# First two groups of a causal convolution on TensorE: x as the stationary operand in 128x32 tiles, written already transposed, and a reordered second bundle

## The chip, the cores and the metric

The kernel runs on one NeuronCore of a Trainium2 chip. The metric is device microseconds of one execution. TensorE is called PE in the profile (PEld is its weight load), VectorE DVE, ScalarE ACT, GpSimd POOL and SyncE SP.

## The reference

The input x is 8 sequences of 4160 tokens with 192 channels, in fp32. Two things are computed one after the other.

```python
# 1. a causal depthwise convolution of 7 taps; the 24 channels of a head share its softmaxed taps
w = softmax(weight, axis=-1)                       # (8 heads, 7)
y[b, s, h*24+g] = sum_k w[h, k] * x[b, s-6+k, h*24+g]
# 2. a channel mix on y
y_prev = y shifted by one token
xk = mu_k*y + (1-mu_k)*y_prev ;  xr = mu_r*y + (1-mu_r)*y_prev
k  = relu(xk @ w_k)            # 192 -> 1024
v  = (k*k) @ w_v               # 1024 -> 192
r  = sigmoid(xr @ w_r)         # 192 -> 192
out = r * v
```

## The kernel before

**Pairs and channels.** The eight sequences go in four pairs. In the transposed activations (`yT`) the 128 partitions hold 64 channels of the one sequence and 64 of the other, so that the 192 channels are three chunks c of 64 (`Q`), and the tokens run along the free dimension.

**Convolution.** Tokens go in blocks of 120. With 126 rows of x behind it, a block's output for one head is a product with a banded 128x128 matrix `toe[:, h, :]`, which holds the softmaxed taps. Blocks are gathered in groups. Pair 0 has groups 0 to 5 of 3, 4, 4, 5, 10 and 9 blocks; the other pairs have four groups each. For all groups the banded matrix is PE's stationary operand (lhsT) and x streams past it, so the result has tokens on the partitions and has to be transposed:

- groups 0, 1 and 2 are convolved by `conv_small`: 10 matmuls (L321), each for one head's part of one chunk, then three casts out of PSUM (L329) into `y_small`. `tr_first` (group 0, L414 to L422) and `tr` (groups 1, 2 and 3, L390) transpose 120x120 blocks on PE and copy them into `yT` (L417, L420, L400);
- group 3 is convolved in two units (`conv_mm`, L300, and `conv_out`, L345), and transposed by `tr` too;
- all later groups are written to DRAM and read back transposed by DMA (`y_write`, `y_read`).

**Channel mix.** A pair's tokens go in steps; pair 0 starts with a step of 256 tokens (step 0), then seven of 512. For a step, DVE forms `d` (`diff`, L444), and from it xk and xr (`scale` L475 and `add_y` L481; in step 0 xk is one L457 for each chunk). A slot n is `k_mm` (L501; six matmuls of 64x512, three chunks by two sequences, or in step 0 twelve of 64x256), `k_relu` on ACT (L530) and `k_square` on DVE (L544). Four slots are a bundle: bundle 0 is step 0, bundles 1 and 2 are step 1, and so on. From bundle 2 on each bundle also has one `r` (L575 and a sigmoid, L583) and one quad of the V product in two halves (`v_rows`, L603), with the product `v_out` (L619) and its DMA.

**Order.** It is written out by hand: each engine runs its instructions in the order in which the program calls them. `prologue` loads, builds `toe` and convolves groups 0 and 1; `bundle_first` is bundle 0; `bundle_rest` is every other bundle. Work that accompanies a bundle hangs in tables by bundle number (`first`, `mix_a`, `mix_b`, `mix_c`, `rq`, `xt`, `late`, `early`). All PSUM tiles are of two banks and come from one ring of four (`ring`): a tile can be taken when one of the last four has been read out. In `conv_mm` and `v_rows` an empty ACT instruction (`clobber_nop`, L308, L611) after the first half keeps ACT from going on before that half is done. x comes through POOL's DMA queue into three buffers `xb`.

Of the kernel before, what the change touches and what calls it, by code (L numbers as in the profile page):

```python
# [7 lines left out]
FP32 = mybir.dt.float32  # L8
# [6 lines left out]
def kernel(  # L15
# [293 lines left out]

    def conv_small(g, copies):  # L310

        nb = groups[g][2]
        ys[g] = [two.tile([P, 4, P], BF16, tag=f"y_small{i}", name="y_small") for i in range(NC)]
        tiles = [ring.tile([P, 2, BANK], FP32, tag="k", name="ps_c") for _ in range(3 if g == 0 else 2)]
        banks = [t[:, i, 0 : nb * P] for t, i in ((tiles[0], 0), (tiles[1], 0), (tiles[-1], 0 if g == 0 else 1))]
        for i, o in enumerate(banks):
            o = o.rearrange("p (n s c) -> p n s c", n=nb, s=2)
            c0, c1 = i * Q, (i + 1) * Q
            for h in range(c0 // G, -(-c1 // G)):
                a, b = max(c0, h * G), min(c1, h * G + G)  # L320
                nc.tensor.matmul(  # L321
                    out=o[:, :, :, a - c0 : b - c0],
                    lhsT=toe[:, h, :],
                    rhs=xbs[g][:, :nb, :, a:b],
                    start=True,
                    stop=True,
                )
        for i, o in enumerate(banks):
            copies[i](out=ys[g][i][:BLK, :nb, :].rearrange("p n c -> p (n c)"), in_=o[:BLK, :])  # L329

# [50 lines left out]
    def tr(g, j):  # L381
# [14 lines left out]
        for i in todo[::2]:  # L396
            n = min(2, nb - i)
            c0 = YC + (blk0 + i) * BLK
            copy = nc.scalar.copy if g == 1 and i > 0 else nc.vector.tensor_copy
            copy(  # L400
                out=yTs[p][:, :, c0 : c0 + n * BLK].rearrange("p c (n t) -> p c n t", n=n),
                in_=view[:, (i - 4 * j) // 2, :, :n, :],
            )

    def tr_first():

        nb = groups[0][2]
        n = nb * BLK
        new_yT(0)
        tiles = [ring.tile([P, 2, 2 * BANK], BF16, tag="k", name="ps_t") for _ in range(2)]  # L410
        for c in range(3):
            for i in range(nb):
                c0 = c % 2 * n + i * BLK
                nc.tensor.transpose(  # L414
                    out=tiles[1 - c // 2][:, 0, c0 : c0 + BLK], in_=ys[0][c][:BLK, i, :], identity=ident[:BLK, :BLK]
                )
        nc.scalar.copy(out=yTs[0][:, 2, YC : YC + n], in_=tiles[0][:, 0, 0:n])  # L417
        for c in range(3):
            if c < 2:
                nc.vector.tensor_copy(out=yTs[0][:, c, YC : YC + n], in_=tiles[1][:, 0, c * n : (c + 1) * n])  # L420
            diff(0, slice(c, c + 1))
            mix(0, 0, slice(c, c + 1))  # L422

# [61 lines left out]
    def k_mm(n, cs=range(NC)):  # L485
# [10 lines left out]
        for c in cs:  # L496
            for f in range(nf):
                fs = slice((j * nf + f) * P, (j * nf + f + 1) * P)
                for i in range(2):
# [7 lines left out]
                    )  # L507

    def k_section(ns):
        s, _ = slots[ns[0]]  # L510
        if ns[0] > 0:
            for n in ns:
                k_mm(n)
            return
        for n in ns:
            k_ps[n] = ring.tile([P, 2, BANK], FP32, tag="k", name="ps_k")
            if n == 0:

                warm(k_ps[0], 3)
        for c in range(NC):  # L520
            if c == NC - 1:
                run(first, 0)
            for n in ns:
                k_mm(n, (c,))

# [124 lines left out]

    early, first, rq, xt, mix_a, mix_b, mix_c, vq, late = ({} for _ in range(9))

    def at(table, b, fn, *a):
        table.setdefault(b, []).append((fn, a))

    def conv(g, c):
        act_, dve_ = nc.scalar.copy, nc.vector.tensor_copy
        conv_small(g, (act_, act_, dve_ if g == 0 else act_))

# [6 lines left out]
    for g, (p, blk0, nb, fb, on_pe) in enumerate(groups):  # L666
        nx = 1 if g < 3 else len(conv_units(g))
        if g == 0:
            continue
        if g == 1:  # L670
            xs = []
        elif p == 0:
            xs = {2: [0], 3: [1, 1], 4: [2, 2, 3, 3], 5: [4, 4, 5, 5]}[g]
        else:
            xs = range(fb - 10, fb - 10 + nx)
        for i, b in enumerate(xs):
            if g == 2:
                at(late, b, conv, g, i)
            else:
                xt.setdefault(b, []).append((g, i))  # L680
        if on_pe:
            for j in range((nb + 3) // 4):
                at(first, g - 1, tr, g, j)
        else:
            at(late, xs[-1], y_write, g)

            at(late, xs[-1] + (1 if g < 6 else 2), y_read, g)
        if g > 4:

            b = {5: 1, 6: 2, 7: 7}.get(g)  # L690
            b = first_bundle[first_step[p]] + (-15, -11, -7, -3)[(g - 6) % 4] if b is None else b
            at(early, b, x_tile, g)
            at(early, b, load_x, g)
    for s, (p, t0, L, n0, ns) in enumerate(steps):
        fb = first_bundle[s]
        if s == 0:
            at(mix_c, 1, mix, s, 1)
            continue
        if s == 1:
            at(mix_a, 0, diff, s)  # L700
            at(mix_a, 0, mix, s, 0)
            at(mix_a, 1, scale, s, 1, 0)
            at(mix_b, 1, scale, s, 1, 1)
            at(late, 2, scale, s, 1, 2)
            at(late, 2, add_y, s, 1)
        else:
            if s == 2:
                at(mix_b, 1, diff, s)
            elif s == 4:
# [31 lines left out]
    def prologue():  # L741
# [33 lines left out]
        load_mu(1, moe_mu_r)  # L775
        conv(0, 0)
        tr_first()
        conv(1, 0)
        x_tile(3)
        load_x(3)  # L780
        load_wr()
        x_tile(4)
        load_x(4)
        load_wv()

    def bundle_first(ns):
        for part in (ns[:2], ns[2:]):
            k_section(part)
            for n in part:
                k_relu(n)  # L790
        run(mix_a, 0)
        for n in ns:
            k_square(n)
        run(late, 0)

    def bundle_rest(b, ns):

        units = xt.get(b, []) + [None, None]
        quad = vq.get(b, [None])[0]
        for n in bundles[b - 1][2:] if b > 1 else ():  # L800
            k_square(n)
        run(mix_a, b)
        k_mm(ns[0])
        k_relu(ns[0])
        run(first, b)
        k_square(ns[0])
        run(mix_b, b)
        conv_half(units[0], 0)
        k_mm(ns[1])
        conv_half(units[0], 1)  # L810
        k_relu(ns[1])
        k_square(ns[1])
        run(rq, b)
        if quad:
            v_rows(*quad, 0)
        k_mm(ns[2])
        k_relu(ns[2])
        conv_half(units[1], 0)
        if quad:
            v_rows(*quad, 1)  # L820
            conv_half(units[1], 1)
        run(mix_c, b)
        k_mm(ns[3])
        if not quad:
            conv_half(units[1], 1)
# [5 lines left out]
    with tc.manual_schedule():  # L831
        prologue()
        for b in range(-20, 0):
            for table in (early, first, rq, xt, mix_a, mix_b, mix_c, vq, late):
                assert b not in table, b
        for b in range(quads[-1][2] + 1):
            run(early, b)
            if b == 0:
                bundle_first(bundles[b])
            elif b < len(bundles):  # L840
                bundle_rest(b, bundles[b])
# [39 lines left out]
```

## Time and profile before

| what | us |
|---|---|
| median of 3 runs | 422.44 (422.27 to 422.84) |
| the profiled execution, as timed | 422.14 |
| its span in the trace | 420.4 |
| PE busy | 409.8 (97%) |
| DVE busy | 380.9 (91%) |
| ACT busy | 347.5 (83%) |

Busy shares are of the span. PE's ends are modelled, so that busy time is time with matmuls in flight. In the groups, a line shows the busy time, the mean of one instruction, and the idle time in front of them with what ended it.

### The profile page before, as it was taken

Reading aid. Unit: us, or ns where it says so; the run is one execution under the profiler, and the core shown is the slowest. Engines: PE = TensorE matmul, PEld = TensorE weight load, DVE = VectorE, ACT = ScalarE, POOL = GpSimd, SP = SyncE. Lnnn points to the kernel's source line nnn. Section 1 sums busy time; section 2 is a strip of 40 time slices with the busy share of each in tenths; the row PEclk is TensorE's granted clock in tenths of the full one; section 3 lists DMA queues with packets and bytes.
Section 4 is the critical chain, followed back from the end, with each engine's and each line's share of the span. In section 5 each row is a group of like instructions: output and inputs, shape, how many; then the busy total and the mean of one; then the engine's idle time right before and its main releaser. Section 6 shows DMA issues by size and latency. Waiting matters only on the chain.

```text
span 420.4 us, 15787 instructions
## 1 busy us (share of the span) xinstructions
PE 409.8 (97%) x6845; PEld 315.7 (75%) x6845; DVE 380.9 (91%) x677; ACT 347.5 (83%) x408; POOL 49.0 (12%) x73
## 2 busy tenths in 40 slices
PE   8789999999999999999999999999999999999995
PEld 3456777777977787777778777877777788777795
DVE  5899889998999999999999999999999999999973
ACT  5788988988888898889888888988898788787771
POOL 7650010202020010202003010201100000000000
PEclk9999999999999999999999999999999999999999
DMA  8996869969599793868769794696856484421123
GB/s 131 192 190 113 217 173 146 227 189 164 165 169 217 152 223 99 139 188 183 182 114 201 167 203 126 140 234 150 160 139 133 138 153 121 118 77 53 64 79 113
DMA packets 134886, 64.58 MB, mean 154 GB/s; under 512 B 85132, under 2 KB 134816, under 8 KB 134816
## 3 DMA queue, kind: packets, MB, share of 16 engines
q1 hardware_dynamic: 96050, 48.31, 45.3%
q0 software_dynamic: 37872, 14.66, 30.4%
q8 instruction: 53, 0.87, 0.8%
q10 hardware_dynamic: 894, 0.61, 0.5%
q14 instruction: 17, 0.14, 0.1%
HBM read 29.92 MB, written 36.99 MB: 159 GB/s over the span
## 4 chain that ended last, share of the span: by engine, by line
PE 90%; ACT 2%; DVE 1%; issue 0%; ACTq 0%
PE ps_v L603 39%; PE ps_k L501 38%; PE ps_r L575 7%; PE ps_c L300 4%; ACT k_sb L530 2%; PE ps_v L558 1%; DVE o_sb L619 0%; ACT y L345 0%; DVE k L544 0%; DVE yT L400 0%; DVE d L444 0%; DVE xr L475 0%; PE ps_t L390 0%; DVE o_sb L639 0%; ACTq L345 0%
## 5 line engine op out<-in xcount | busy, mean ns | idle before, releaser
L530 ACT ACTIVATE k_sb<-ps_k 128x1024 bf16<-128x1024 f32 x260 | 261.3, 1040 | 52.5 <-PE ps_k L501 52.5
L501 PE MATMUL ps_k<-xk,wk 64*128 64x512 bf16 (+1 forms) x1632 | 201.0, 367 | 1.5 <-ACT k_sb L530 0.5
L544 DVE TENSOR_TENSOR k<-k_sb 128x1024 bf16<-128x1024 bf16 x260 | 177.6, 687 | 14.9 <-ACT k_sb L530 7.8
L603 PE MATMUL ps_v<-wv,k 64*128 64x192 bf16 x4032 | 188.8, 243 | 0.2 <-ACT y L345 0.2
L603 PEld LDWEIGHTS <-k 64*128 64x128 bf16 x4032 | 172.5, 94 | 13.2 <-issue 0.7
L501 PEld LDWEIGHTS <-wk 64*128 64x128 bf16 x1632 | 87.8, 94 | 52.2 <-issue 2.5
L619 DVE TENSOR_TENSOR o_sb<-ps_v,r_sb 128x768 f32<-128x768 f32 x64 | 61.2, 956 | 11.9 <-PE ps_v L603 5.0
L583 ACT ACTIVATE r_sb<-ps_r 128x768 bf16<-128x768 f32 x65 | 54.7, 845 | 0.0
L345 ACT CAST y<-ps_c 120x960 bf16<-120x960 f32 (+4 forms) x67 | 50.9, 789 | 4.5 <-PE ps_c L300 4.5
L125 POOL DMA_DIRECT2D xb<-in_x_dram x34 | 30.7, 905 | 195.3 <-PE ps_c L300 129.3
L575 PEld LDWEIGHTS <-xr 64*128 64x128 bf16 x780 | 35.9, 94 | 11.3 <-DVE yT L400 0.4
L575 PE MATMUL ps_r<-wr,xr 64*128 64x192 bf16 x780 | 43.8, 243 | 0.0
L300 PE MATMUL ps_c<-xb,toe 64*128 64x480 bf16 (+2 forms) x240 | 39.5, 335 | 0.1
L475 DVE TENSOR_SCALAR xr<-d,mu 128x512 bf16<-128x512 bf16 (+1 forms) x102 | 35.5, 351 | 0.0
L475 DVE TENSOR_SCALAR xk<-d,mu 128x512 bf16<-128x512 bf16 (+1 forms) x99 | 32.6, 358 | 0.1
L481 DVE TENSOR_TENSOR xr<-xr,yT 128x1536 bf16<-128x1536 bf16 (+1 forms) x33 | 31.0, 939 | 1.1
L444 DVE TENSOR_TENSOR d<-yT 128x1536 bf16<-128x1536 bf16 (+2 forms) x35 | 31.0, 887 | 1.0 <-ACT yT L400 0.8
L481 DVE TENSOR_TENSOR xk<-xk,yT 128x1536 bf16<-128x1536 bf16 (+1 forms) x32 | 30.2, 942 | 0.0
L300 PEld LDWEIGHTS <-toe 64*128 64x128 bf16 x240 | 13.4, 94 | 12.2 <-DVE o_sb L619 0.5
L428 POOL COPY y_tail<-yT 128x195 bf16<-128x195 bf16 x4 | 1.8, 458 | 68.5 <-DMA yT<-y_dram 68.5
L739 PE MATMUL warm<-zeros,ones_t 128*128 128x512 bf16 x16 | 6.5, 594 | 1.8 <-DVE zeros L754 1.8
L739 PEld LDWEIGHTS <-ones_t 128*128 128x128 bf16 x19 | 2.6, 135 | 5.6 <-issue 4.0
(55 smaller groups left out, 63.9 us busy)
## 6 DMA issues: line engine op xcount, KB each, us to landing
out_dram<-o_sb SPq DMA_DIRECT2D x128, 192.0 KB, 2.6
y_dram<-y SPq DMA_DIRECT2D x10, 900.0 KB, 6.7
xb<-in_x_dram POOLq DMA_DIRECT2D x14, 480.0 KB, 9.1
xb<-in_x_dram POOLq DMA_DIRECT2D x6, 432.0 KB, 7.6
xb<-in_x_dram POOLq DMA_DIRECT2D x10, 192.0 KB, 4.9
y_dram<-y SPq DMA_DIRECT2D x3, 450.0 KB, 5.7
y_dram<-y SPq DMA_DIRECT2D x1, 810.0 KB, 5.8
wk<-in_moe_w_k_dram POOLq DMA_DIRECT2D x4, 192.0 KB, 7.0
```

The costliest lines, as they stand in the source:

```text
L300: nc.tensor.matmul(out=banks[:, bank, :, :, k * G : (k + 1) * G], lhsT=toe[q, h, :], rhs=xbs[g][q, :nb, :, h * G : (h + 1) * G], start=hal ...
L345: copy(out=bass.AP(tensor=y.tensor, offset=y.offset + d0, ap=[y.ap[0], [d1 - d0, 2], [2 * D, nb], [Q, 2], [1, n]],), in_=bass.AP(tensor=ps ...
L444: nc.vector.tensor_tensor(out=shaped(s, diffs[s][:, cs, :L]), in0=y_of(s, cs, 1), in1=y_of(s, cs, 0), op=ALU.subtract)
L475: nc.vector.tensor_scalar(out=t[:, c, :L], in0=diffs[s][:, c, :L], scalar1=mu[:, i, c : c + 1], scalar2=None, op0=ALU.mult)
L481: nc.vector.tensor_tensor(out=o, in0=o, in1=y_of(s, sl, 0), op=ALU.add)
L501: nc.tensor.matmul(out=ps[:, i, f * L : (f + 1) * L], lhsT=wk[r, c, fs], rhs=xk[r, c, :L], start=c == 0 and f == 0, stop=c == NC - 1 and f ...
L530: nc.scalar.activation(out=k_sb, in_=ps.rearrange("p a b -> p (a b)"), func=AF.Relu)
L544: nc.vector.tensor_tensor(out=o, in0=i, in1=i, op=ALU.mult)
L575: nc.tensor.matmul(out=ps[:, i, k * D : (k + 1) * D], lhsT=xr[q, c, ts], rhs=wr[q, c, :], start=c == 0, stop=c == NC - 1,)
L583: nc.scalar.activation(out=r_sbs[s, j], in_=ps[:, :, 0 : 2 * D], func=AF.Sigmoid)
L603: nc.tensor.matmul(out=v_ps[s, j][:, bank, k * D : (k + 1) * D], lhsT=k2s[s][q, f, t * P : (t + 1) * P], rhs=wv[q, f, :], start=half == 0 ...
L619: nc.vector.tensor_tensor(out=o_sb.rearrange("p (b t) d -> p b (t d)", b=2), in0=v_ps.pop((s, j)), in1=r_sbs.pop((s, j)), op=ALU.mult,)
```

## The change

Groups 0 and 1 are convolved by the new `conv_t`. There x is the stationary operand, 32 columns at a time, and the banded matrix streams: each matmul takes 128 rows of one block of x and 32 channels of one sequence, and writes 32 PSUM partitions by 120 tokens, which is a piece of `yT` as it has to lie. The four pieces (two sequences by two halves of a chunk) write the four quarters of the partitions. Where 32 channels cross a head's border, a second, narrower matmul (8, 16 or 24 columns) writes over the first channels. So there are 8 matmuls for each block and chunk: 72 for group 0 and 96 for group 1. `to_yT` copies a chunk's PSUM to `yT` on ACT. `tr_first`, the `conv_small` of these groups, group 1's `tr` and three `warm` matmuls in bundle 0 go away. The queue of group 0's mixing on DVE stays, chunk by chunk; step 1's `diff` and xk are made chunk by chunk too.

Bundle 1 gets an order of its own (`bundle_second`): group 2's convolution stands after the second slot, its casts are spread (two on ACT between slots, one on DVE), and group 2's transposes and group 3's convolution follow the last slot. Group 3's transposes move into bundle 2, between the first half of its V product and its third slot; bundle 2's two convolution units move behind the third slot. wv is loaded ahead of group 4's x; group 7's x is loaded a bundle later; the part of xr that is made in bundle 1 is placed anew.

```diff
+    def conv_t(g, c, o, blocks):
+        for n, i in enumerate(blocks):
+            for first_piece in (True, False):
+                for s in range(2):
+                    for q in range(2):
+                        c0 = c * Q + q * 32
+                        lo, hi = c0 // G, (c0 + 31) // G
+                        h, m = (hi, 32) if first_piece else (lo, hi * G - c0)
+                        p0 = s * Q + q * 32
+                        nc.tensor.matmul(
+                            out=o[p0 : p0 + m, n * BLK : (n + 1) * BLK],
+                            lhsT=xbs[g][:, i, s, c0 : c0 + m],
+                            rhs=toe[:, h, 0:BLK],
+                            start=True,
+                            stop=True,
+                        )
+
+    def to_yT(g, c, o, b0, b1, copy):
+        c0 = YC + (groups[g][1] + b0) * BLK
+        copy(out=yTs[0][:, c, c0 : c0 + (b1 - b0) * BLK], in_=o[:, 0 : (b1 - b0) * BLK])
...
-            copy = nc.scalar.copy if g == 1 and i > 0 else nc.vector.tensor_copy
-            copy(
+            nc.vector.tensor_copy(
...
-    def tr_first():
...
-    def k_section(ns):
...
-            b = {5: 1, 6: 2, 7: 7}.get(g)
+            b = {5: 1, 6: 2, 7: 8}.get(g)
...
-            at(mix_c, 1, mix, s, 1)
+            at(mix_a, 1, mix, s, 1)
             continue
         if s == 1:
-            at(mix_a, 0, diff, s)
-            at(mix_a, 0, mix, s, 0)
-            at(mix_a, 1, scale, s, 1, 0)
-            at(mix_b, 1, scale, s, 1, 1)
+            at(mix_b, 1, scale, s, 1, 0, 1)
...
             if s == 2:
-                at(mix_b, 1, diff, s)
+                at(mix_c, 1, diff, s)
...
         load_mu(1, moe_mu_r)
-        conv(0, 0)
-        tr_first()
-        conv(1, 0)
         x_tile(3)
         load_x(3)
         load_wr()
+        load_wv()
         x_tile(4)
         load_x(4)
-        load_wv()
 
     def bundle_first(ns):
-        for part in (ns[:2], ns[2:]):
-            k_section(part)
-            for n in part:
-                k_relu(n)
-        run(mix_a, 0)
+        new_yT(0)
+        tiles = [ring.tile([P, 2, BANK], FP32, tag="k", name="ps_t") for _ in range(2)]
+        for n, (g, c) in enumerate((g, c) for g in range(2) for c in range(NC)):
+            o = tiles[n % 2][:, n // 2 % 2, :]
+            conv_t(g, c, o, range(groups[g][2]))
+            to_yT(g, c, o, 0, groups[g][2], nc.scalar.copy)
+            if g == 0:
+                diff(0, slice(c, c + 1))
+                mix(0, 0, slice(c, c + 1))
+
+        for c in range(NC):
+            for n in ns[:2]:
+                k_mm(n, (c,))
+        for n in ns[:2]:
+            k_relu(n)
+        for c in range(NC):
+            diff(1, slice(c, c + 1))
+            mix(1, 0, slice(c, c + 1))
+        for n in ns[2:]:
+            k_mm(n)
+            k_relu(n)
         for n in ns:
             k_square(n)
         run(late, 0)
 
+    def bundle_second(b, ns):
+        act_, dve_ = nc.scalar.copy, nc.vector.tensor_copy
+        k_mm(ns[0])
+        k_relu(ns[0])
+        k_mm(ns[1])
+        cast = conv_small(2)
+        cast[0](act_)
+        k_relu(ns[1])
+        cast[1](act_)
+        cast[2](dve_)
+        k_mm(ns[2])
+        k_relu(ns[2])
+        k_mm(ns[3])
+        k_square(ns[0])
+        run(mix_a, b)
+        tr(2, 0)
+        conv_half(xt[b][0], 0)
+        k_relu(ns[3])
+        conv_half(xt[b][0], 1)
+        k_square(ns[1])
+        run(mix_b, b)
+        conv_half(xt[b][1], 0)
+        conv_half(xt[b][1], 1)
+        run(mix_c, b)
+        run(late, b)
...
     def bundle_rest(b, ns):
...
-        run(first, b)
         k_square(ns[0])
         run(mix_b, b)
-        conv_half(units[0], 0)
+        if b > 2:
+            conv_half(units[0], 0)
         k_mm(ns[1])
-        conv_half(units[0], 1)
+        if b > 2:
+            conv_half(units[0], 1)
...
             v_rows(*quad, 0)
+        if b == 2:
+            tr(3, 0)
+            tr(3, 1)
         k_mm(ns[2])
         k_relu(ns[2])
-        conv_half(units[1], 0)
-        if quad:
-            v_rows(*quad, 1)
-            conv_half(units[1], 1)
+        if b == 2:
+            conv_half(units[0], 0)
+            v_rows(*quad, 1)
+            conv_half(units[0], 1)
+            conv_half(units[1], 0)
+        else:
+            conv_half(units[1], 0)
+            if quad:
+                v_rows(*quad, 1)
+                conv_half(units[1], 1)
         run(mix_c, b)
         k_mm(ns[3])
-        if not quad:
+        if not quad or b == 2:
             conv_half(units[1], 1)
```

## The prediction

> **What bounds the kernel now.** I read the engines' busy time first, then the chain that ended last, then busy time by stage.
>
> ```profile
> PE 409.8 (97%) x6845; PEld 315.7 (75%) x6845; DVE 380.9 (91%) x677; ACT 347.5 (83%) x408; POOL 49.0 (12%) x73
> PE 90%; ACT 2%; DVE 1%; issue 0%; ACTq 0%
> ```
>
> The first line is PE's share of the span, the second its share of the chain. By stage:
>
> ```profile
> 8.00:14.70 6.70, 6.47 (x82) 4.32 (x81) 4.63 (x14) 3.48 (x8) 4.83 (x7) 1.00 1.37 188
> 14.70:33.20 18.50, 14.82 (x197) 9.32 (x198) 16.57 (x34) 15.76 (x21) 7.92 (x12) 1.00 1.59 190
> 33.20:60.00 26.80, 26.48 (x438) 19.44 (x436) 23.51 (x41) 24.93 (x31) 0.00 (x0) 1.00 0.73 173
> 60.00:400.00 340.00, 340.00 (x5846) 265.53 (x5842) 320.24 (x553) 289.92 (x335) 29.61 (x41) 1.00 0.75 154
> ```
>
> The stage rows give stretch, length, and busy us of PE, PEld, DVE, ACT, POOL. From 33.2 us on PE leaves 0.3 us idle in 367. Whatever moves the start of that phase moves the end by as much; nothing later can win it back or lose it. Between 14.7 and 33.2 PE has 3.7 us idle, and ACT (15.8 of 18.5) and DVE (16.6) set the pace. So the question is when PE reaches one fixed point of the program. I take the first matmul of n12 (bundle 3's first slot): by then both orders have done the same work, but for one unit's second half (0.2 us), and their queues agree after it. In the timeline of before n11 and n12 are one row:
>
> ```profile
> 12.68 0.80 PE L390 MATMUL ps_t<-ident,y_small 120*128 120x120 bf16 x12
> ...
> 14.74 3.78 ACT L530 ACTIVATE k_sb<-ps_k 128x1024 bf16<-128x1024 f32 x4
> ...
> 18.36 1.61 ACT L329 CAST y_small<-ps_c 120x512 bf16<-120x512 f32 x3
> ...
> 28.91 1.48 PE L603 MATMUL ps_v<-wv,k 64*128 64x192 bf16 x32
> ...
> 32.60 1.46 PE L501 MATMUL ps_k<-xk,wk 64*128 64x512 bf16 x12
> ```
>
> A pair takes (1.46 - 0.38)/5 = 0.214, the last matmul's 0.38 taken off, so n12 starts at 32.60 + 3 x 0.214 = 33.24. I call slot n's relu Rn. R0 starts at 14.74; four relus in 3.78, the last taking 1.06, are one each 0.91 us.
>
> **Cost of conv_t.** It adds 168 matmuls of 120 columns, 42 sets of four. No tile of 32 columns is in the trace, so I bound a set from three rows. L390: 12 matmuls of 120 columns in 0.80 us, 0.22 each, start 0.053 apart. L603 (two tiles of 64 rows) starts one per (1.48 - 0.24)/31 = 0.040 us, and the same 192 columns over the whole array one per 0.083:
>
> ```profile
> 410.31 5.45 PE L558 MATMUL ps_v<-wv,k 128*128 128x192 bf16 x64
> ```
>
> So tiles of different rows run side by side. If those of different columns do too, a set takes 0.053 (all 42: 2.2 us), which is also the least, since each quarter must stream its 120 columns. If they run in line, it takes 0.212 (8.9 us). Between them lies the shortest step seen between two matmuls with a weight load each, 0.029 us (L321 behind a 48-column one): 0.116 a set, 4.9 us. I take 0.053, by L603 as the only row with tiles; the others set the range.
>
> The Trainium skill speaks for and against. "TensorEngine Tiling (Array Packing)", section Key Properties, says that different tiles load and multiply in parallel; L603 agrees for rows. The same page, Restrictions and Gotchas, says that column tiling excludes the fast weight load, and "TensorE: Matmul & The Clock Gate", section LDWEIGHTS, puts a load at its columns over 1.2 GHz: as an estimate 27 ns for 32 columns, hidden if the four load together, 107 ns a set in line. By the latter the sum below would be a gain of 1.7 us rather than 2.8; no row here shows such a load.
>
> **Bundle 0.** conv_t starts at 8.13, as L321 did (ACT's cast of x ends there). Group 0's 18 sets end at 9.08. Group 1's x landed at 9.59 (issued at 3.28), so its 24 sets run to 10.86. In the way of the first slots stands wk: its first half landed at 11.43, its second at 13.57. DVE's chain for xk: chunk 0's copy on ACT 8.62 to 9.08 (0.46, as L417), `diff` 0.29, L457 0.49, so 9.9; the chunks follow at 10.65 and 11.4. All three are there when wk is; in before the third was ready at 12.80. Then n0 and n1, 12 pairs of 256 columns at 0.107, from 11.45; n0 is complete at 12.68: R0 12.70, R1 13.6. n2 waits for wk (13.57) and is complete at 14.35: R2 14.5, R3 15.45, next ACT slot 16.36. In before these four ran from 14.74, behind a copy of group 1's transposes (L400, 14.08 to 14.84), and three casts of group 2 followed them. Of what went, `tr_first` and group 1's `tr` took PE, ACT and DVE off this path; the three `warm` matmuls (0.8 us of PE) lay in a wait and are worth nothing.
>
> DVE makes step 1's xk by chunks: an add of 512 columns about 0.43 (between 0.29 for 256 and 0.96 for 1536), so 1.24 a chunk, 3.7 us against 2.88 in one piece. But it starts at 11.4, not at 14.87, and ends at 15.2, not 17.75. This 0.8 us more hides behind R1 to R3.
>
> **Bundles 1 and 2.** ACT carries this chain. R4 16.36; first cast 17.3 (0.47 a cast in a row); R5 17.75; second cast 18.65; R6 19.1. n7 takes the tile that R5 frees at 18.8; group 2's transposes (0.65, and 0.1 for the change of tile shape, as between L501 and L390) end at 20.2; the first half of group 3's unit is done at 20.65, and the empty ACT instruction there stands ahead of R7: R7 20.7, 0.55 late, which I count. Then two units' copies (0.9, and 0.3 + 0.6 for the split one), R8 23.35, R9 24.3, the sigmoid 25.2. In before R8 was at 26.31: 2.96 gained here.
>
> From here DVE is later: from group 2's `yT` copies (20.4) it has, without a pause, two copies 1.0, n5's square 0.6, two scalings 0.5, the difference of step 2 0.9, two squares 1.2, a scaling 0.35, a square 0.6, two scalings 0.55, a square 0.6, and group 3's three `yT` copies 1.3: 28.0. The tile for group 4's first unit is free after the second of these, 27.6, while PE could take it at 26.65: a stall of 0.95, counted too. Then that half, the V half (1.3), the other halves, n11 and n12: 30.4. V's first half runs at 23.6 to 24.95; group 3's transposes, that stalled PE by 0.9 us at 25 in before, lie behind it.
>
> **Loads.** POOL's queue now has wv before group 4's x. The bytes are the same, and the last of them landed at 26.92; wv should come at about 22 (V wants it at 23.6) and group 4's x at 27 (wanted at 27.6). Group 3's x waits for conv_t on group 0 (9.3) instead of L329's casts (9.62), no later; landed 19.4, wanted 20.25. Each cover is 0.6 to 1.6 us; what a load is late beyond it, PE stalls. Group 7's x, one bundle later, has two bundles of 6.14 us to its convolution, and such loads landed in 9.1: nothing. Its DVE write and POOL's issues keep their order. SP's queue is unchanged.
>
> **Sum.** 33.24 - 30.4 = 2.84 us. The profiled execution took 422.14 with a span of 420.4: 419.3, span 417.6. The median of the runs shown is 0.30 above it: 419.6.
>
> **Rivals.**
> - *A floor of 0.029 us for each load and matmul.* conv_t ends at 8.13 + 42 x 0.116 = 13.0; R0 and all behind it move by 1.55. Gain 1.3, time 421.1. For it: 336 small instructions on a path where no row shows a shorter step for a whole-height load. Against: L603's pairs. Up to 0.077 a set ((11.43 - 9.59)/24) the wait for wk hides everything.
> - *The quarters run in line* (slower). conv_t ends at 17.0, R0 slips by 5.6, n12 to 36.0: 2.7 us lost, 425.2. The sum turns at 14.3 for conv_t's end, 0.147 a set. For it: every tile here has the same 128 rows, and only tiles of different rows are seen together.
> - *PE's clock falls back.* The 16 warm matmuls start 0.43 us apart until 7.3 and then 0.22, so PE has a slow state, though the page's granted clock stands at 9 tenths or more throughout. Without the extra warm ones and with PE half idle until 11.4, bundle 0's slots would take 5.1 instead of 2.57: R3 1.4 us later, up to 2.6 with bundle 1: 421.0 to 422.2. Against: PE stayed fast through transposes and gaps from 8 to 18.
>
> **Numbers.** Likeliest case 0.50, floor 0.26, in line 0.16, clock 0.06, something else 0.02. A measurement of this kernel can tell about 0.2% (0.8 us) from no change. Faster by more: nearly all of the first case, most of the second (up to 0.127 a set), a little of the fourth: 0.70. Within: the rest of the second and third near the turn: 0.12. Slower 0.18. Range: down to 418.7, if DVE's 0.95 us stall does not come; up to 423.4, a set of 0.19, which leaves about 0.12 above and 0.06 below.
>
> **What would show it.** Right: in the changed profile, conv_t's 168 matmuls lie within 2.8 us from 8.13; the first k_mm at about 11.45, R0 at 12.7, R8 at 23.4, n12 at 30.4 (each within 0.5), and no idle PE after. Wrong: conv_t reaching past 13; first slots spaced 0.2 us a pair; PE waiting for group 4's x or wv; or n12 early and PE idle after 33.

## The result, and the profile after

The changed kernel took 423.0 us (422.87 to 423.14), the kernel before in the same series 422.6 (422.27 to 422.84). The ratio is 1.001 [0.9993, 1.0027], which is no change that can be measured. The profiled execution of the changed kernel took 422.87 us with a span of 421.2, against 422.14 and 420.4 before. The forecast was 419.6, with a span of 417.6.

The page, with the engines' shares, the queue that brings instructions, and the chain that ended last:

```profile
PE 408.3 (97%) x6969; PEld 315.5 (75%) x6969; DVE 380.0 (90%) x678; ACT 346.7 (82%) x406; POOL 48.9 (12%) x73
...
q8 instruction: 54, 0.88, 0.9%
...
PE 86%; DMA 3%; ACT 2%; issue 1%; DVE 0%; ACTq 0%
```

PE is busy 1.5 us less than before and yet the span is 0.8 us longer. In the chain "issue" has gone from 0% to 1%: PE waited for nothing that the profile can name. By stage, in the columns of the prediction:

```profile
8.00:14.70 6.70, 5.78 (x207) 4.37 (x206) 5.91 (x19) 4.60 (x9) 4.44 (x7) 1.00 1.40 192
14.70:33.20 18.50, 15.42 (x202) 10.07 (x202) 15.50 (x33) 14.02 (x18) 8.21 (x12) 1.00 1.60 191
33.20:60.00 26.80, 26.02 (x434) 19.58 (x431) 22.09 (x39) 24.51 (x31) 0.00 (x0) 1.00 0.71 170
60.00:400.00 340.00, 339.49 (x5829) 264.16 (x5827) 319.98 (x554) 289.68 (x335) 29.61 (x41) 1.00 0.74 154
```

Two things stand out. In the stretch from 14.7 to 33.2 no engine is near full: PE idles 3.1 us, ACT 4.5 (2.7 before) and DVE 3.0 (1.9 before), so they wait for each other. And after 33.2, where PE left 0.3 us idle before, it leaves 1.3. PE's timeline (start, length, instructions of one row, and in brackets the idle time in front with what ended it):

```profile
7.90 0.98 PE L320 MATMUL ps_t<-toe,xb 128*32 128x120 bf16 x48 [0.87 <-DVE toe L268]
9.12 2.35 PE L320 MATMUL ps_t<-toe,xb 128*32 128x120 bf16 x120 [0.24 <-ACT yT L330]
11.40 1.86 PE L507 MATMUL ps_k<-xk,wk 64*128 64x256 bf16 x25
13.74 0.94 PE L507 MATMUL ps_k<-xk,wk 64*128 64x256 bf16 x14 [0.47 <-DMA wk<-in_moe_w_k_dram]
14.96 2.00 PE L507 MATMUL ps_k<-xk,wk 64*128 64x256 bf16 x21 [0.29 <-issue]
...
29.40 0.38 PE L300 MATMUL ps_c<-xb,toe 64*128 64x480 bf16 x2 [1.62 <-DVE yT L425]
...
32.20 0.82 PE L507 MATMUL ps_k<-xk,wk 64*128 64x512 bf16 x6
...
113.50 0.49 PE L592 MATMUL ps_v<-wv,k 64*128 64x192 bf16 x7 [0.45 <-issue]
```

The first two rows are conv_t: 168 matmuls, done at 11.47. n12 (the row at 32.20) comes 1.04 us earlier than before, not 2.84. Its unit in front, group 4's first, waited 1.62 us for DVE's copies of group 3. The row at 14.96 and the one at 113.50 follow pauses that have no releaser. DVE's timeline leads back to where those copies became late:

```profile
16.88 0.69 DVE L533 TENSOR_TENSOR k<-k_sb 128x1024 bf16<-128x1024 bf16 x1 [0.15 <-ACT k_sb L519]
17.79 0.06 DVE L105 MEMSET xb<- 1x1 uint32 x1 [0.21 <-PE ps_c L343]
19.68 0.69 DVE L351 CAST y_small<-ps_c 120x512 bf16<-120x512 f32 x1 [1.84 <-ACT y_small L351]
20.29 0.68 DVE L533 TENSOR_TENSOR k<-k_sb 128x1024 bf16<-128x1024 bf16 x1
20.89 0.78 DVE L481 TENSOR_SCALAR xr<-d,mu 128x256 bf16<-128x256 bf16 x3
21.71 0.56 DVE L487 TENSOR_TENSOR xr<-xr,yT 128x768 bf16<-128x768 bf16 x1
22.19 0.96 DVE L425 COPY yT<-ps_t 128x720 bf16<-128x720 bf16 x2
...
28.38 1.21 DVE L425 COPY yT<-ps_t 128x720 bf16<-128x720 bf16 x3
```

The row at 22.19 is group 2's copies, the one at 28.38 group 3's. DVE, which the prediction let start this chain in time, stood still 1.84 us in front of its cast of group 2's third chunk, until ACT had made its own cast of the second chunk. Both read one PSUM tile, each another bank of it: the changed kernel puts the three chunks at `((tiles[0], 0), (tiles[1], 0), (tiles[1], 1))`. ACT's timeline:

```profile
19.00 0.66 ACT L351 CAST y_small<-ps_c 120x512 bf16<-120x512 f32 x1
...
27.81 1.02 ACT L519 ACTIVATE k_sb<-ps_k 128x1024 bf16<-128x1024 f32 x1 [0.91 <-PE ps_k L507]
31.34 2.01 ACT L371 CAST y<-ps_c 120x960 bf16<-120x960 f32 x2 [2.50 <-PE ps_c L300]
```

ACT's cast at 19.00 ends at 19.66 and DVE's begins at 19.68. PE's last eight transposes of group 2 waited for DVE's cast:

```profile
20.43 0.59 PE L416 MATMUL ps_t<-ident,y_small 120*128 120x120 bf16 x8 [0.45 <-DVE y_small L351]
```

Eleven microseconds later the delay is part of what ACT waits: 2.50 us idle in front of group 4's first copy (31.34). The waits of the first stages say the same in one list, and one more line stands in the waits after 33 us:

```profile
ACT y L371 <- PE ps_c L300: 2.5, 1, 2.5
PEld L300 <- DVE yT L425: 2.1, 1, 2.1
DVE y_small L351 <- ACT y_small L351: 1.8, 1, 1.8
...
PEld L300 <- DMA xb<-in_x_dram: 0.6, 1, 0.6
```

To follow a gain to the end I use the start of each V product on DVE (`o_sb`, L608, 64 in all), taken against its counterpart before. The changed kernel is at -1.47 in quad 0, -0.42 in quads 2 and 3, about -0.15 from quad 8, and +0.51 from quad 14 (after the pause at 113 us); the last one starts at 413.63 instead of 413.16, +0.47.

### The profile page after: what moved, and what is told of

Read it like the earlier page. It is cut to its first block, busy times and chain, and to the rows that moved or that the text cites. A ratio compares the mean times of both kernels' runs of the same rounds, so it can differ in the third digit from the quotient of the medians.

```text
span 421.2 us, 16034 instructions
## 1 busy us (share of the span) xinstructions
PE 408.3 (97%) x6969; PEld 315.5 (75%) x6969; DVE 380.0 (90%) x678; ACT 346.7 (82%) x406; POOL 48.9 (12%) x73
## 4 chain that ended last, share of the span: by engine, by line
PE 86%; DMA 3%; ACT 2%; issue 1%; DVE 0%; ACTq 0%
PE ps_v L592 38%; PE ps_k L507 36%; PE ps_r L564 7%; PE ps_c L300 4%; DMA xb<-in_x_dram 3%; ACT k_sb L519 1%; PE ps_v L547 1%; ACT y L371 0%; DVE o_sb L608 0%; DVE yT L425 0%; DVE o_sb L628 0%; ACTq L371 0%; ACTq L308 0%; ACTq L600 0%
## 5 line engine op out<-in xcount | busy, mean ns | idle before, releaser
L608 DVE TENSOR_TENSOR o_sb<-ps_v,r_sb 128x768 f32<-128x768 f32 x64 | 61.2, 957 | 12.1 <-PE ps_v L592 5.3
L450 DVE TENSOR_TENSOR d<-yT 128x1536 bf16<-128x1536 bf16 (+3 forms) x37 | 31.3, 847 | 1.3 <-DMA yT<-y_dram 0.9
L487 DVE TENSOR_TENSOR xk<-xk,yT 128x1536 bf16<-128x1536 bf16 (+2 forms) x34 | 30.5, 896 | 0.1
L713 PE MATMUL warm<-zeros,ones_t 128*128 128x512 bf16 x16 | 5.2, 498 | 1.8 <-DVE zeros L728 1.8
L107 POOL MEMSET xb<- 32x384 bf16 x3 | 1.2, 407 | 48.2 <-PE ps_k L507 44.3
```

The costliest lines, as they stand in the source:

```text
L450: nc.vector.tensor_tensor(out=shaped(s, diffs[s][:, cs, :L]), in0=y_of(s, cs, 1), in1=y_of(s, cs, 0), op=ALU.subtract)
L487: nc.vector.tensor_tensor(out=o, in0=o, in1=y_of(s, sl, 0), op=ALU.add)
L608: nc.vector.tensor_tensor(out=o_sb.rearrange("p (b t) d -> p b (t d)", b=2), in0=v_ps.pop((s, j)), in1=r_sbs.pop((s, j)), op=ALU.mult,)
```

## The experiments

Each series has its own runs of the kernel before on the same chip; a ratio is against those. Three explanations were weighed first. A: the delay sits in the new order of bundles 1 and 2 (DVE's cast behind ACT's, and what follows from it). B: an early start of the long phase is given back later whatever the order. C: the pauses without a releaser, which come with the new instruction stream, eat the gain. Before, in the first series, took 422.91 (421.99 to 424.48), in the second 422.76 (421.84 to 423.75), in the third 422.74 (421.88 to 425.23).

### conv_t alone

conv_t, `to_yT` and the new bundle 0; from bundle 1 on the old order, loads and tables.

```diff
-        conv(0, 0)
-        tr_first()
-        conv(1, 0)
...
+            conv_t(g, c, o, range(groups[g][2]))
+            to_yT(g, c, o, 0, groups[g][2], nc.scalar.copy)
```

> Groups 0 and 1 by conv_t, everything from bundle 1 on in the order of before, loads as before. Theory A (conv_t wins what was forecast, and the new order of bundles 1 and 2 loses it through two waits on DVE): R0 at 13.1 instead of 14.7, R4 about 1.6 us earlier than in before (18.2), the first V product (o_sb) 1 to 1.6 us earlier than 32.66, and the median 0.8 to 1.6 us below before. Rival B (ACT and DVE pace everything up to 45 us, so a faster start is given back whatever the order): o_sb of the third quad at 46.2 as in before, median within 0.3 us of before. Rival C (PE's longer instruction stream, 248 rows more, makes it pause later): a pause of PE of 0.3 to 0.6 us with no wait somewhere after 60 us, near 113 us as in the changed kernel.

Measured: 421.55 us, ratio 0.9961 [0.9942, 0.9979]. The V products lie at -1.03 from quad 0 to quad 12 without a change, and at -0.29 after a pause of PE of 0.68 us at 112.68. So conv_t by itself gains, and in the old order nothing is given back between 25 and 110 us: B falls. C holds in part: of 1.03 us the pause takes 0.7, and in bundle 0 this kernel has 1.04 us of "issue" at its 447th PE instruction (matmuls and weight loads counted in order of start).

### The order alone

The old convolution of groups 0 and 1, with `bundle_second`, the new bundle 2, the new load order and mixing.

```diff
+            elif b == 1:
+                bundle_second(b, bundles[b])
...
+            b = {5: 1, 6: 2, 7: 8}.get(g)
```

> Groups 0 and 1 convolved and transposed as in before, bundles 1 and 2 and the loads in the new order. Theory A: R0 at 14.7, the DVE cast of group 2 waits 1 to 2 us for ACT's cast, group 4's first unit waits for group 3's copies, and the median is 0.5 to 1.5 us above before. Rival B: within 0.3 us of before. Rival C: no pause of PE near 113 us, as PE has as many instructions as before.

Measured: 425.24 us, 1.0058 [1.0037, 1.0078]: 2.3 us slower than before, more than any theory had. PE's and DVE's waits from 8 to 34 us:

```profile
PE ps_k L526 <- DVE xk L506: 2.1, 1, 2.1
PE ps_c L300 <- DVE yT L425: 1.8, 1, 1.8
...
DVE y_small L350 <- ACT y_small L350: 1.5, 1, 1.5
```

The third line is the cast wait again, the second the wait of group 4's first unit that follows from it; the first is this kernel's own (it was 0.5 in the kernel before): step 1's xk, which the old convolution delivers late, now has a slot of bundle 1 waiting for it at 17.6. The order is thus made for an early xk, and even with one it carries the cast wait. The V products lie at +0.5 in quad 0, at +1.55 from quad 2 and at +1.8 after a pause at 114.6.

### The cast in its own tile

The changed kernel with one difference: chunks 0 and 1 of group 2, both cast by ACT, share the first tile, and DVE's chunk has the second to itself.

```diff
-((tiles[0], 0), (tiles[1], 0), (tiles[1], 1))
+((tiles[0], 0), (tiles[0], 1), (tiles[1], 0))
```

> The changed kernel, but the third chunk of group 2's convolution has a PSUM tile of its own, so that DVE's cast doesn't follow ACT's. Theory A: DVE's 1.8 us of idle before this cast (17.85 to 19.68) falls below 0.3, group 2's transposes end 0.5 to 0.8 us earlier, group 4's first unit starts 0.8 to 1.5 us earlier than 29.40, n12 0.6 to 1.2 us earlier than 32.20; median 0.5 to 1.0 us below the changed kernel's. Rival B: n12 earlier, but the third quad's o_sb at 45.8 all the same and the median within 0.2 us of the changed kernel's. Rival C: the PE pause of 0.6 us near 113 us stays.

Measured: 420.64 us, 0.9932 [0.9912, 0.9952], 2.3 us below the kernel before in its series, where the changed kernel was 0.4 above in its own. DVE's timeline:

```profile
18.30 0.69 DVE L351 CAST y_small<-ps_c 120x512 bf16<-120x512 f32 x1 [0.33 <-issue]
```

and PE's:

```profile
15.48 2.00 PE L507 MATMUL ps_k<-xk,wk 64*128 64x256 bf16 x21 [1.18 <-issue]
...
28.26 0.38 PE L300 MATMUL ps_c<-xb,toe 64*128 64x480 bf16 x2 [0.74 <-DVE yT L425]
...
31.06 0.82 PE L507 MATMUL ps_k<-xk,wk 64*128 64x512 bf16 x6
```

DVE no longer waits for ACT: its cast starts 1.38 us earlier, group 4's first unit and n12 1.14 earlier, though the pause of bundle 0 (the row at 15.48) is longer here (1.45 us between starts of matmuls, against 0.56). The wait came from the shared tile. It is an order that the program asks for: in the trace of the changed kernel DVE's cast carries a wait for the semaphore that ACT raises, and with a tile of its own it carries none on ACT. ACT's cast of the first chunk (18.07 to 18.66) runs beside it. The kernel before could have shown the way: there group 0's three chunks have a tile each, and ACT's second cast and DVE's overlap:

```profile
8.49 0.86 ACT L329 CAST y_small<-ps_c 120x384 bf16<-120x384 f32 x2 [0.42 <-PE ps_c L321]
...
9.12 0.56 DVE L329 CAST y_small<-ps_c 120x384 bf16<-120x384 f32 x1 [0.39 <-PE ps_c L321]
```

That the end improves by 2.2 in the trace and not by 1.1 has two further reasons: the pause at 113 us (0.61) did not occur, and neither did PE's wait for group 7's x at 79.6 (0.22).

### Group 3's transposes later

`tr(3, 0)` and `tr(3, 1)` go from the front of bundle 2's third slot to the end of the bundle, so that group 4's first unit does not stand behind their copies.

```diff
-        if b == 2:
-            tr(3, 0)
-            tr(3, 1)
         k_mm(ns[2])
...
             conv_half(units[1], 1)
+        if b == 2:
+            tr(3, 0)
+            tr(3, 1)
```

> The changed kernel, but group 3's transposes and their copies stand behind bundle 2's last slot and second unit instead of between V's first half and the third slot. Theory A: group 4's first unit starts at 27.8 instead of 29.40, ACT's idle 2.5 us in front of its copy falls below 0.7, n12 0.8 to 1.5 us earlier than 32.20; median 0.5 to 1.2 us below the changed kernel's. Rival B: n12 earlier, third quad's o_sb at 45.8, median as the changed kernel's. Rival C: the PE pause near 113 us stays.

Measured: 421.61 us, 0.9953 [0.9934, 0.9972]. ACT's timeline, then n12 in PE's and its relu in ACT's:

```profile
28.79 2.01 ACT L371 CAST y<-ps_c 120x960 bf16<-120x960 f32 x2 [0.86 <-PE ps_c L300]
...
31.66 0.82 PE L507 MATMUL ps_k<-xk,wk 64*128 64x512 bf16 x6 [0.49 <-DVE yT L425]
...
32.52 1.02 ACT L519 ACTIVATE k_sb<-ps_k 128x1024 bf16<-128x1024 f32 x1 [0.79 <-PE ps_k L507]
```

The unit comes 2.5 us earlier (26.85) and ACT's idle time before its copy falls from 2.50 to 0.86. But n12 starts at 31.66, only 0.54 us earlier than in the changed kernel: it stands behind the transposes' copies (0.70), and the gate's matmuls wait 0.66 us for xr, which is made from the same copies. The V products are at -1.0 from quad 2, 0.6 earlier than the changed kernel's, then at -0.5 after a pause of 0.43 at 112.47. So most of what the unit gained went into new waits ahead of n12, and the rest of it, about 0.5, reached the end.

### More instructions ahead, and the pause inside conv_t

The shared-tile remedy, and in place of the 16 warm matmuls of 512 columns, 80 of 48 columns and 4 of 512. This tests whether the pause of bundle 0 belongs to a place in PE's instruction stream.

```diff
-        warm(ring.tile([P, 2, BANK], FP32, tag="k", name="warm"), WARM)
+        w = ring.tile([P, 2, BANK], FP32, tag="k", name="warm")
+        small(w, 80)
+        warm(w, 4)
```

> The kernel of e3 (DVE's cast from a tile of its own), with PE's 16 warm matmuls of 512 columns replaced by 80 of 48 columns and 4 of 512: 136 more PE instructions in the time before conv_t, none after. Theory A now has a second part: PE stands still for 0.6 to 1.5 us at its 447th instruction in every kernel with conv_t (14.96, 15.73, 15.48, 15.21 us), with no wait, because its instruction fetch of 16 KB (256 instructions) does not follow the run of 168 small matmuls. With the first 16 KB used up before conv_t starts, the fetch comes early: no pause over 0.3 us between 13 and 17 us, bundle 0's last relu 0.5 to 1 us earlier than in e3, n12 0.3 to 1.2 us earlier than 31.06, median 0.3 to 1.2 us below e3. Rival: the pause is PE's own (clock, or the change of tile shape) and stays at the same matmul of bundle 0; or it lies beside ACT's work, and the median stays within 0.2 us of e3.

Measured: 424.45 us, 1.0043 [1.0028, 1.0058], slower. PE's timeline:

```profile
11.31 0.23 PE L320 MATMUL ps_t<-toe,xb 128*32 128x120 bf16 x3 [0.23 <-ACT yT L330]
13.69 0.96 PE L320 MATMUL ps_t<-toe,xb 128*32 128x120 bf16 x29 [2.14 <-issue]
```

The pause, 2.37 us long, has moved into conv_t. Counted in PE's instructions it has stayed: in front of the 446th here, in front of the 447th in the changed kernel and in all others that have conv_t and a pause. So it depends on the position in the stream and not on which matmul stands there. The records of the queue that brings instructions fit: it moves packets of 16 KB. One starts at 12.57 in the changed kernel, at 11.46 here and at 12.91 with the cast in its own tile, in the kernels with this pause 2.6 to 3.5 us after about the 191st instruction, and PE goes on 2.2 to 2.6 us after the packet's start. The remedy was mis-sized: 167 instructions stand ahead of conv_t here, so the one that brings the packet lies in conv_t's fast run and not ahead of it.

### Group 7's load back in its place

The cast in its own tile, and group 7's x loaded a bundle earlier, as before.

```diff
-            b = {5: 1, 6: 2, 7: 8}.get(g)
+            b = {5: 1, 6: 2, 7: 7}.get(g)
```

> The kernel of e3 with group 7's x loaded at bundle 7 again. Theory: the later load costs only where it lands late; it landed at 79.53 in the changed kernel and PE waited 0.2 us, and in e3 there was no such wait. So the median is within 0.3 us of e3 and no PE wait for that load appears. Rival: the earlier load takes DMA time from others, and the time goes up by over 0.3 us.

Measured: 420.9 us, 0.9958 [0.9942, 0.9975], the same as without this edit (0.9932 in its own series) within the intervals. There is no wait for x, but that kernel had none either. Its V products keep about -2.05 to quad 12, and then a pause of 0.61 us at 111.61 takes it to -1.43. The edit is worth at most the 0.22 us that the wait cost in the changed kernel. This kernel is also the cleanest measure of the cast: it has both pauses, as the changed kernel has, and after the first of them PE goes on at the same 14.96 us. PE's timeline:

```profile
14.96 2.00 PE L507 MATMUL ps_k<-xk,wk 64*128 64x256 bf16 x21 [0.72 <-issue]
...
30.54 0.82 PE L507 MATMUL ps_k<-xk,wk 64*128 64x512 bf16 x6
```

From there n12 comes 1.66 us earlier than in the changed kernel (32.20). In one series the two take 420.9 and 422.88 us (the latter below).

### All remedies so far at once

Cast in its own tile, group 3's transposes late, group 7's load back.

> The kernel of e3 with group 3's transposes behind bundle 2's last unit (as in e4) and group 7's x at bundle 7. Theory A: e3 still has PE wait 1.1 us for group 3's copies in front of group 4's first unit; without that n12 comes 0.3 to 0.9 us earlier than 31.06 and the median is 0.3 to 0.9 us below e3. Rival B: in e4 the late transposes put a new wait into bundle 3 (0.66 us for xr, 0.7 us for the copies); if these come back the median is as e3 or up to 0.6 us above.

Measured: 421.71 us, 0.9976 [0.9966, 0.9985]. Less than the cast alone: the first unit starts at 27.07, but n12's wait for the copies (0.70) and the gate's for xr (0.66, at 34.24) are back as in the kernel with late transposes only, and wk's second half landed late here (PE waited for it to 14.81). The late transposes are no help once the cast is in time.

### The changed kernel again

No edit; in the series of the last three, as a reference.

> The changed kernel as it is, once more, beside the others. The wait of DVE's cast for ACT's (1.8 us) and of group 4's first unit for group 3's copies (about 2 us) come back within 0.2 us; so does the pause at the 447th PE instruction. If the pause of 0.6 us at 113.5 us is chance in the fetch, it may be missing or of another length; if it belongs to the program's position it is there again.

Measured: 422.88 us, 1.0012 [0.9995, 1.0028]. The delays of bundles 0 to 2 and the later pause return: 1.74 us in front of DVE's cast, 1.74 in front of group 4's first unit, a pause of 0.60 at the 447th PE instruction and one of 0.55 at 113.26. These belong to the kernel and not to one execution. The wait for group 7's x does not return: the second half of this load landed 8.56 us after its issue, against 11.09, and the V products keep -0.33 up to the pause.

### Enough instructions ahead

The cast in its own tile, and 100 matmuls of 24 columns and 6 of 512, so that 212 instructions stand ahead of conv_t.

```diff
-        small(w, 80)
-        warm(w, 4)
+        small(w, 100)
+        warm(w, 6)
```

> The kernel of e3 with the 16 warm matmuls replaced by 100 of 24 columns and 6 of 512 (212 PE instructions ahead of conv_t instead of 32). In e5 the pause moved to the same place in the instruction stream (446th instruction, then in the middle of conv_t), not with the matmul; from a fetch's first packet to PE's next matmul it was 2.2 to 2.6 us in every run, and that packet came 2.5 to 3.4 us after about the 191st instruction. Theory A: with the 191st instruction before 6 us, the fetch starts before 9 us and PE has instructions again by 11.5 us; the 447th is then reached at about 11 us: pause below 0.6 us (0.6 to 1.45 in e3 and its kind, 2.4 in e5), and no second pause before 20 us. Median 0 to 0.8 us below e3. Rival: the fetch's start hangs on something else, and the pause comes at the 447th instruction with 1 to 2.4 us; the median is then 0.5 us or more above e3.

Measured: 420.77 us, 0.9955 [0.9935, 0.9976], span 418.6. PE's timeline:

```profile
11.38 0.60 PE L320 MATMUL ps_t<-toe,xb 128*32 128x120 bf16 x32 [0.23 <-ACT yT L330]
11.92 4.50 PE L507 MATMUL ps_k<-xk,wk 64*128 64x256 bf16 x60
```

Sixty matmuls stand in one row without a pause. The 16 KB packet now starts at 8.03, and n12 at 30.62, where 30.4 was forecast. In the trace this is 0.4 us less span than the cast alone; in the medians (0.9955 here, 0.9932 in another series) no difference can be told.

### The copies ahead of a square

The cast in its own tile, and in bundle 2 the square of the second slot behind `tr(3, 1)`, so that DVE copies group 3's transposes first.

```diff
-        k_square(ns[1])
...
         tr(3, 1)
+        k_square(ns[1])
```

> The kernel of e3 with the square of bundle 2's second slot put behind group 3's yT copies on DVE (0.6 us that stood ahead of them). Theory A: group 4's first unit waits 0.5 us instead of 1.1 (28.26 in e3 becomes 27.7), n12 0.4 to 0.7 us earlier than 31.06, median 0.3 to 0.7 us below e3. Rival B: ACT and DVE pace bundle 3 anyway; n12 earlier, third quad's o_sb and median within 0.2 us of e3.

Measured: 420.52 us, 0.9943 [0.9923, 0.9964]. PE's timeline:

```profile
27.62 0.38 PE L300 MATMUL ps_c<-xb,toe 64*128 64x480 bf16 x2 [0.19 <-DVE yT L425]
...
30.43 0.82 PE L507 MATMUL ps_k<-xk,wk 64*128 64x512 bf16 x6
```

0.64 us are gained at the unit (28.26 with the cast alone) and 0.63 at n12, and nothing becomes late for it. The V products are at -2.20 in quads 2 and 3 and at -1.98 from quad 5; a pause of 0.42 at 111.5 takes them to -1.54.

### The order alone, with the cast mended

The old convolution with the new order, and the cast in its own tile.

> The kernel of e2 (old convolution of groups 0 and 1, new order of bundles 1 and 2) with DVE's cast from a tile of its own. Theory A: the wait for ACT's cast (1.5 us in e2) goes and the median falls 1 to 2 us below e2's, to 0 to 1 us above before: the new order is worth something only once conv_t has freed the time before it. Rival: the order is bad in itself and the median stays over 1.5 us above before.

Measured: 423.87 us, 1.0022 [1.0007, 1.0038]. This is 1.4 us less than the order alone, though still above the kernel before. Its main wait stands where it was:

```profile
PE ps_k L526 <- DVE xk L506: 2.1, 1, 2.1
...
PE ps_c L300 <- DVE yT L425: 0.7, 1, 0.7
```

PE's wait for group 3's copies went from 1.8 to 0.7, that for step 1's xk did not move. It also has a pause of 0.67 us at 113.74 without any conv_t. So the mended order needs conv_t's early xk: neither part gains alone what they gain together.

### The cast, the instructions ahead and the copies

The three edits that each helped in the trace.

> The kernel of e3 with the edits of e9 and e10 together. Theory A: if both hold, n12 1 to 1.5 us earlier than in e3 and the median 0.5 to 1.3 us below e3 (419.4 to 420.2). Rival: only the larger of the two is seen.

Measured: 420.07 us (419.31 to 421.13), 0.9937 [0.9918, 0.9957]; the profiled execution took 419.35, with a span of 417.6. Its stages from 14.7 us on:

```profile
14.70:33.20 18.50, 16.87 (x228) 11.12 (x226) 17.80 (x37) 16.31 (x21) 8.19 (x12) 1.00 1.60 191
33.20:60.00 26.80, 26.43 (x437) 19.85 (x433) 22.63 (x40) 24.11 (x31) 0.00 (x0) 1.00 0.78 183
60.00:400.00 340.00, 340.00 (x5872) 265.88 (x5869) 320.66 (x557) 290.61 (x336) 29.73 (x41) 1.00 0.73 154
```

and PE's timeline:

```profile
27.00 0.38 PE L300 MATMUL ps_c<-xb,toe 64*128 64x480 bf16 x2
...
29.80 0.82 PE L507 MATMUL ps_k<-xk,wk 64*128 64x512 bf16 x6
```

Between 14.7 and 33.2 us DVE now works 17.8 of 18.5 us and PE 16.9 (15.4 in the changed kernel). Group 4's first unit has no wait in front of it. From 60 to 400 us PE is never idle. The span is the 417.6 that was forecast, but not by the forecast's way: n12 is 0.6 us earlier than its 30.4, and as much is lost behind it. This version beats the kernel before by 2.7 us and the changed kernel by about as much. That it is also faster than the cast alone is seen only in the trace (417.6 against 419.0), not in the medians.

## Why the prediction was wrong

**conv_t's rate was right, its length was not.** A set of four was put at 0.053 us by the only row with tiles. In the trace one set follows the other by 0.052, for narrow second pieces too, and neighbours start 0 to 5 ns apart but for one step of about 49 in each four, or two of about 15 and 30 in some chunks. The loads take 82 to 97 ns each, for 8 columns as for 32 (the estimate was 27), and lie beside the matmuls. The Trainium skill's "TensorEngine Tiling (Array Packing)", section Key Properties, holds here for columns as well; the loss of the fast weight load that its section Restrictions and Gotchas names cost no time that could be seen at 120 columns. The rivals that priced a set at 0.116 or 0.212 are false, and so is the one on PE's clock: from 11.9 on bundle 0's pairs start 0.109 us apart and not 0.2, and the granted clock was 1.00 in every stage. But the 168 matmuls end at 11.47, 3.3 us after 8.13, where the prediction allowed 2.8. It left out that from the third chunk on each chunk starts 0.05 us after the end of an ACT copy out of the tile that it writes into (9.12 after 9.06, 9.48 after 9.43, 10.17 after 10.12, 10.87 after 10.81). This cost next to nothing, since wk landed at 11.73.

**The step that failed** is the one on bundles 1 and 2: "group 2's `yT` copies (20.4)". They start at 22.19. The working takes them from the end of group 2's transposes and gives times to ACT's two casts alone; DVE's cast of the third chunk stands nowhere in it, so its wait was put at nothing without a reason. In fact it stood 1.84 us behind ACT's cast from the same PSUM tile, until 19.68. DVE then had the cast, a square, three scalings and an addition ahead of the copies, 2.5 us; without the wait it would have come to them at 20.4 (17.84 and 2.5), as forecast. From there the sum went as it was written: the chain on DVE that it put at 7.6 us took 7.4, group 3's copies ended at 29.59 instead of 28.0, group 4's first unit came at 29.40 instead of 27.6, n12 at 32.20 instead of 30.4. Of the 1.80 us that n12 was late, the shared tile is 1.66: n12 stands at 30.54 with the cast in its own tile and group 7's load back, where PE goes on after the pause of bundle 0 at 14.96, as in the changed kernel. With the cast alone it stands at 31.06, but there PE goes on 0.52 later, at 15.48. With no pause in bundle 0 it stands at 30.62, so a pause as short as the changed kernel's does not show in n12. The last 0.14 is not traced.

**"Nothing later can win it back or lose it"** failed too, and it gave away most of what was left. Three terms:

- n12 was no point of equal work for ACT. ACT was 0.42 us ahead there, not 1.04 (its relu of n12 at 34.15 against 34.57), and PE came back to ACT's pace in small waits between 33 and 43 us. Four other kernels of the new order lose the same amount: 2.18 us ahead at n12 and 1.56 at the V products of quads 2 and 3 with the cast alone, 2.62 and 2.0 with the instructions ahead, 2.81 and 2.20 with the copies first, 3.44 and 2.82 with all three; in the changed kernel 1.04 and 0.42. It is 0.61 or 0.62 each time.
- The load of group 7's x was priced "nothing", by a cover of two bundles (12.3 us) and loads that landed in 9.1. Its second half was issued 10.9 us before PE wanted it and landed in 11.09, so PE waited 0.22. A single load spreads widely: the same half took 13.06 us in the kernel before, and 8.56, without a wait, when the changed kernel ran again. That it cost something in this profile is chance.
- At 113.50 PE paused for 0.61 us, with no releaser. The old program has no such pause, and no step of the prediction looked at how instructions reach PE.

Together with about 0.3 us after the last V product (outputs that land later) the account closes: 1.80 + 0.62 + 0.22 + 0.61 + 0.3 = 3.55, and the span was 421.2 - 417.6 = 3.6 above the forecast.

**The relus** were 0.4 us late against the forecast in bundle 0 (R0 13.08, not 12.70) and 0.9 at R8 (24.21, not 23.35). wk's first half landed at 11.73 instead of 11.43, the pause at the 447th instruction stood in the second pair of slots, and R7 came at 21.55, behind the transposes that waited for DVE's cast. No wait for wv or for group 4's x shows, as the prediction had it.

**The range** reached up to 423.4, and 423.0 lies inside it by luck: that end stood for a slow conv_t, which did not come. Its sum is also wrong: by the prediction's own rule a set of 0.19 gives 424.3, and 423.4 goes with 0.17. What did come is the prediction's last sign of being wrong, n12 early and PE idle after 33.

**What is open.** The pauses stand at fixed positions of PE's instruction stream: the 447th instruction, and near the 3509th, which is 447 and about 12 times 256 (256 is an estimate: 54 packets in the instruction queue and 13,938 matmuls and loads in the program make 258 a packet, if they are all PE's); and the kernel that has 248 fewer PE instructions ahead of it (the mended order without conv_t) pauses 257 earlier. That a packet of instructions comes late is the likely reason, from the times of the packets; it was not shown by itself. Why the later pause is missing in the kernel with the cast alone, whose stream is the same, is not settled: its packet started at 108.2 us, at the 3380th instruction, against 111.1 and the 3432nd in the changed kernel.

## What to carry to other kernels

When an instruction moves to another engine, ask not only whether that engine has time but what else reads the buffer that it reads: two banks of one tile, emptied by two engines, were emptied one after the other, because the program held a wait by tile, and this one wait decided between no change and a gain of 2 us (422.88 against 420.9 in one series). When a gain is measured at one point of the program, take the other engines' positions at that point as well, since the one that lags takes its part back. A change that helps a stage can need another to pay: here the new order lost alone and gained only behind the early xk of the new convolution (with the cast mended, the V products of quads 2 and 3 are at -1.56 in the trace, against -1.03 with conv_t alone).

## What the runs showed of the hardware

- Four matmuls of 128x32 tiles, each with its own load of weights, ran side by side at 0.052 us a set of 120 columns, neighbours starting 0 to 5 ns apart but for one step of about 49 in each four, or two of about 15 and 30.
- A run of short PE instructions can meet a pause that no wait explains: 0.5 to 2.4 us at the 447th instruction, where conv_t ran some 170 matmuls and as many loads in 3.5 us. With 212 instructions ahead of conv_t it did not occur.
- A similar pause of 0.2 to 0.7 us came at 111 to 115 us in eight of the fourteen profiles, two of them without conv_t. What sets it off is open.
